# Building the decay masks and the query factors on the chip instead of loading them

## The chip, the cores and the metric

The kernel runs on one core of a Trainium2 chip. The metric is the device time of one execution in microseconds (us), lower is better. A profile of one execution gives the span of the core's work, engine by engine: PE is TensorE (its weight loads stand apart as PEld), DVE is VectorE, ACT is ScalarE, POOL is GpSimd, SP is the engine whose queue issues most DMAs. ACT has a DMA queue of its own.

## What is computed

The input is one attention-like layer ("retention": no softmax, a decay per head) and two feed-forward layers behind it, all in float32.

```python
# q, k, v: 4 batches x 8 heads x 576 positions x 64
gamma = 1.0 - 2.0 ** (-5.0 - arange(8))               # one decay per head
rel = pos[:, None] - pos[None, :]
Dmat = where(rel >= 0, gamma[:, None, None] ** rel, 0.0)
x = ((q @ k.T) / sqrt(64) * Dmat) @ v                 # 2304 tokens x 512
h = x @ w_in;   x = maximum(0.01 * h, h) @ w_out      # 512 -> 2048 -> 512
h = x @ w_in2;  x = (h - tanh(h)) @ w_out2
```

## The kernel before

The first stage, `retention()`, takes about the first 150 us; the two feed-forward layers, `layers()`, take the rest. Everything below on the change lies in the first 30 us of `retention()`.

The 8 heads are taken two at a time, so there are 4 batches x 4 pairs of heads = 16 steps, which this text numbers 0 to 15; step i uses head pair i mod 4. A step cuts the 576 positions into four chunks of 128 and a tail of 64. Within a chunk it forms the scores k.q (`scores`, L595, tile `sc`), multiplies them by the causal decay mask of the two heads (`mask`, L609, on DVE, into `pt`), and multiplies by v (`outputs_near`, L671). What earlier chunks contribute goes through a running state: k times v per chunk (`states_mm`, L628, tile `x_c`; k is first scaled by `kt_sb` in `prep_k`, L576, on ACT), added up with the heads' decay on DVE (`states`, L636 and L638), and multiplied by q (`outputs_far`, L660), where q has been multiplied by its own decay factors `qt_sb` in `prep_q` (L565 and L570, on POOL). The tail's scores are L601 and its mask L618.

The constants come from the host as three tables: the masks `cmask` (128 x 4 pairs x 2 x 128 floats, 128 KB a pair), q's factors `qtab` (64 KB a pair) and `ktab` (4 KB). Pair 0's part of the first two is loaded on ACT's queue at the start, the parts of pairs 1 to 3 on SP's queue in steps 0 to 2, ahead of the loads of q, k and v (L827, L828).

The order on each engine is the order in which the code is written (the schedule is manual), and every engine runs its instructions in that order. A DMA completes on one of eight semaphores, taken in turn; the issue of a DMA whose semaphore is still in use waits for the earlier DMA. There is one `sc` buffer, so the scores of step i+1 wait until DVE has read those of step i. From step 5 on, each step also does a piece of the first feed-forward layer (`unit_h`, L721; `unit_o`, L746). The weights for that are loaded from step 0 on into the not yet used end of `acc` and narrowed from float64 words on ACT, DVE and POOL (`fill`: L152, L158, L163, L169, L242, L243), a few instructions in each step.

A float32 matmul of the program is two records of the trace (8 score products are "x16"), one in the reduced float32r form is one record.

Of the kernel before, what the change touches and what calls it, by code (L numbers as in the profile page):

```python
# [10 lines left out]
F32 = mybir.dt.float32  # L11
# [3 lines left out]
AF = mybir.ActivationFunctionType  # L15
ALU = mybir.AluOpType
PSUM = bass.MemoryType.PSUM

P = 128
CH = 128  # L20
# [15 lines left out]
def retention_moe_moe(  # L36
# [7 lines left out]
    w1o: bass.AP,  # L44
    w2i: bass.AP,
    w2o: bass.AP,
    cmask: bass.AP,
    qtab: bass.AP,
    ktab: bass.AP,
    out: bass.AP,  # L50
    gamma: list,
# [1 line left out]
    nc = tc.nc  # L53
    B, NP, _, S = qT.shape
    NT, DM = out.shape
    NF = w1i.shape[0]
    KK = DM // P
# [21 lines left out]
    acc_t = acc.rearrange("p (d t) -> p d t", d=KK)  # L79
# [15 lines left out]
    QW, EARLY = 256, 6  # L95
# [421 lines left out]
    def retention():  # L517
        with ExitStack() as ac:
            ak = ac.enter_context(tc.tile_pool(name="ak", bufs=1))
# [4 lines left out]
            ps_a = ac.enter_context(tc.tile_pool(name="ps_a0", bufs=1, space=PSUM))  # L524
# [3 lines left out]
            x_b = ps_s.tile([P, 2, QW], F32, name="x_b")  # L528
# [4 lines left out]
            cm_sb = ak.tile([P, NP, 2, CH], F32, name="cm_sb")  # L533
            qt_sb = ak.tile([P, NP, CH], F32, name="qt_sb")
            kt_sb = ak.tile([P, NP, 2], F32, name="kt_sb")
            sts = [ak.tile([P, NFULL, 64], F32, name=f"st{i}") for i in range(2)]
            decay = ak.tile([P, NP], F32, name="decay")
            pt_ = [ak.tile([P, 2, S], F32, name=f"pt{i}") for i in range(2)]
            bds = [ak.tile([P, 2, TAIL], F32, name=f"bd{i}") for i in range(2)]
            qk, kv, pts = {}, {}, {}  # L540
            order = [(b, p) for b in range(B) for p in range(NP)]

            def load(i):
                load_qk(i)
                load_v(i)
# [32 lines left out]
            def prep_tail(i):  # L578

                q = qk[i][:, 1, MAIN:]  # L580
                for h in range(2):
                    o = slice(64 * h, 64 * h + 64)
                    if i:
                        nc.scalar.activation(out=bds[i % 2][o, h, :], in_=q[o], func=AF.Copy)
                    else:
                        nc.vector.tensor_copy(out=bds[i % 2][o, h, :], in_=q[o])
# [109 lines left out]
            def fill(i, part):  # L696
                a, b = marks[i:i + 2] if i < len(order) else marks[-1:] * 2
                now = a + (b - a) * (part + 1) // 3
                for op in ops[done[0]:now]:
                    op()  # L700
                done[0] = max(done[0], now)
# [66 lines left out]
            def pair_steps(i, fast):  # L768

                nonlocal u  # L770
                if fast:
                    unit_h(u)
                    fill(i, 1)
                    if u:
                        unit_o(u - 1)
                        unit_evac(u - 1)
                    u += 1
                if i:
                    ot = o_place(i - 1)
                    outputs_far(i - 1, ot, range(1, NFULL))  # L780
                    outputs_near(i - 1, ot, range(NFULL))
                    outputs_far(i - 1, ot, [NFULL])
                    outputs_near(i - 1, ot, [NFULL])
                    del qk[i - 1]
                    del pts[i - 1], kv[i - 1]
                if i < len(order):
                    states_mm(i)
                    scores_tail(i)
                    states(i)
                if i:  # L790
                    finish(i - 1, x_t, MAIN, S)
                    finish(i - 1, ot[:, :MAIN], 0, MAIN)
                if i < len(order):
                    mask_tail(i)
                if i + 1 < len(order):
                    prep_tail(i + 1)
                    prep_k(i + 1)

            t = ap_.tile([P, 2, S], F32, tag="qk", name="qk")
            nc.sync.dma_start(out=t[:, 1, :], in_=qT[0, 0])  # L800
            nc.scalar.dma_start(out=cm_sb[:, 0], in_=cmask[:, 0])
            nc.sync.dma_start(out=t[:, 0, :], in_=kT[0, 0])
            qk[0] = t
            nc.scalar.dma_start(out=kt_sb, in_=ktab)
            nc.scalar.dma_start(out=qt_sb[:, 0, :], in_=qtab[:, 0, :])
            load_v(0)
            load_qk(1)
            load_v(1)
# [9 lines left out]
            for p in range(NP):  # L818
                for h in range(2):
                    nc.vector.memset(  # L820
                        decay[64 * h:64 * h + 64, p:p + 1], float(gamma[2 * p + h] ** CH)
                    )
            prep_tail(0)
            prep_k(0)
            for i in range(len(order)):
                if i + 1 < NP:
                    nc.sync.dma_start(out=cm_sb[:, i + 1], in_=cmask[:, i + 1])  # L827
                    nc.sync.dma_start(out=qt_sb[:, i + 1, :], in_=qtab[:, i + 1, :])  # L828
                if i + 2 < len(order):
                    load(i + 2)  # L830
                if i < 2:
                    load_piece(pieces[i + 1])
                fast = i >= first
                sc = scores(i)
                prep_q(i)
                mask(i, sc)
                fill(i, 0)
                pair_steps(i, fast)
                fill(i, 2)
            pair_steps(len(order), True)  # L840
            assert done[0] >= len(ops)
# [222 lines left out]
```

## Time and profile before

| | |
|---|---|
| median of 3 runs | 876.88 us (876.71 to 878.21) |
| the profiled execution's own time | 876.76 us |
| its span | 875.0 us |
| PE, busy share of the span | 98% |
| DVE, ACT, POOL, busy share | 67%, 51%, 42% |
| stages | about 150 us retention with pieces of the first layer, then the two layers |

The profile is of one execution, whose own time is 1.76 us longer than its span. In its chain of the work that ended last, PE has 89% of the span. The shares are means over stages: the change touches only the start, which has to be read by itself.

### The profile page before, as it was taken

The numbers are of one execution on the slowest core, as the hardware profiler recorded it, in microseconds if no ns is written. First come the engines' busy times: TensorE is split into PE (matmuls) and PEld (weight loads), VectorE is DVE, ScalarE is ACT, GpSimd is POOL, SyncE is SP. The second block draws the span as 40 slices with busy tenths as digits, with TensorE's granted clock in tenths as the row PEclk, the third lists the DMA queues.
The fourth block names the chain that finished last, engine by engine and source line by source line (L and its number), as shares of the span: only waits on it lengthen the run. The fifth ranks groups of instructions, "written<-read, shape, count | busy, mean of one in ns | idle before, by whom it ended". The sixth has DMA issues, their size and how long they took to land.

```text
span 875.0 us, 14820 instructions
## 1 busy us (share of the span) xinstructions
PE 857.5 (98%) x5584; PEld 744.8 (85%) x5584; DVE 587.6 (67%) x1006; ACT 445.6 (51%) x888; POOL 365.0 (42%) x297
## 2 busy tenths in 40 slices
PE   6999999999999999999999999999999999999997
PEld 5889999888988888888888888888898889889886
DVE  5996776687685777658745567754666566656665
ACT  4553454453345334454534566665666556665663
POOL 2642222140046203273334756554455545453553
PEclk9999999999999999999999999999999999999999
DMA  9835663333455433654534200260004300261112
GB/s 336 316 120 181 207 206 133 133 120 121 145 193 209 153 120 108 230 193 114 208 111 145 97 1 1 73 211 7 1 25 146 119 1 1 73 217 49 49 49 73
DMA packets 36471, 109.23 MB, mean 125 GB/s; under 512 B 4144, under 2 KB 5680, under 8 KB 36400
## 3 DMA queue, kind: packets, MB, share of 16 engines
q1 hardware_dynamic: 35968, 108.08, 35.9%
q8 instruction: 44, 0.72, 0.3%
q10 hardware_dynamic: 432, 0.20, 0.1%
q14 instruction: 27, 0.22, 0.1%
HBM read 78.39 MB, written 29.88 MB: 124 GB/s over the span
## 4 chain that ended last, share of the span: by engine, by line
PE 89%; DVE 5%; DMA 2%; issue 1%; POOL 1%; ACT 1%; SPq 0%; POOLq 0%; DVEq 0%; ACTq 0%
PE a L404 40%; PE h L262 26%; PE h L296 12%; PE a L746 3%; PE x_b L721 3%; PE o L671 1%; DMA cm_sb<-in_cmask 1%; PE sc L595 1%; PE o L660 1%; DVE cw L169 1%; DMA acc<-in_w1i 1%; DVE pt L609 1%; PE x_c L628 0%; DVE acc L467 0%; DVE xl L482 0%
## 5 line engine op out<-in xcount | busy, mean ns | idle before, releaser
L262 PE MATMUL h<-xh,wi 128*128 128x512 f32 (+1 forms) x800 | 229.7, 356 | 0.0
L404 PE MATMUL a<-wp,g 128*128 128x512 f32 x864 | 220.4, 393 | 0.9 <-POOL g L376 0.5
L404 PEld LDWEIGHTS a<-wp,g 128*128 128x128 f32 x864 | 154.5, 188 | 29.5 <-POOL g L376 1.2
L243 POOL TENSOR_TENSOR wi<-cw,wi 128x512 fp32r<-128x512 f32 x64 | 89.8, 1420 | 214.0 <-ACT wi L242 188.3
L404 PE MATMUL a<-g,wp 128*128 128x512 f32 (+1 forms) x816 | 175.9, 364 | 0.6 <-DVE g L376 0.6
L404 PEld LDWEIGHTS a<-g,wp 128*128 128x128 f32 x816 | 141.4, 189 | 25.6 <-DVE g L376 0.8
L262 PEld LDWEIGHTS h<-xh,wi 128*128 128x128 f32 x800 | 143.6, 188 | 22.5
L262 PE MATMUL h<-xl,wi 128*128 128x512 f32 (+1 forms) x400 | 142.4, 356 | 0.0
L350 POOL TENSOR_TENSOR v<-t,u 128x512 f32<-128x512 f32 (+1 forms) x76 | 92.4, 1216 | 92.4 <-ACT t L347 90.5
L376 POOL TENSOR_TENSOR g<-v,g 128x512 fp32r<-128x512 f32 (+1 forms) x76 | 95.7, 1259 | 80.8 <-ACT g L375 80.8
L336 ACT ACTIVATE g<-h 128x512 fp32r<-128x512 f32 (+1 forms) x68 | 37.2, 548 | 166.4 <-PE h L262 124.5
L169 DVE SCALAR_TENSOR_TENSOR cw<-st,cw 128x512 uint32<-128x512 uint32 x112 | 99.0, 884 | 2.9
L370 DVE SCALAR_TENSOR_TENSOR v<-q,v 128x512 f32<-128x512 f32 (+1 forms) x76 | 54.7, 720 | 49.9 <-POOL v L350 49.6
L262 PEld LDWEIGHTS h<-xl,wi 128*128 128x128 f32 x400 | 75.5, 189 | 11.4
L467 DVE TENSOR_TENSOR acc<-a,acc 128x512 f32<-128x512 f32 (+1 forms) x114 | 70.9, 658 | 21.0 <-PE a L404 21.0
L375 ACT ACTIVATE g<-v 128x512 fp32r<-128x512 f32 (+1 forms) x76 | 45.4, 597 | 75.5 <-DVE v L373 68.1
L346 ACT ACTIVATE u<-h 128x512 f32<-128x512 f32 (+1 forms) x80 | 44.0, 550 | 78.0 <-DVE h L290 53.9
L296 PE MATMUL h<-xh,wi 128*128 128x256 f32 x384 | 75.6, 281 | 0.5 <-DVE v L373 0.3
L369 DVE TENSOR_TENSOR h<-h,t 128x512 f32<-128x512 f32 (+1 forms) x80 | 51.5, 644 | 33.7 <-ACT t L347 32.9
L158 DVE TENSOR_SCALAR cw<-cw 128x512 f32<-128x512 f32 x64 | 34.1, 533 | 57.8 <-ACT cw L152 57.7
L296 PEld LDWEIGHTS h<-xe,wi 128*128 128x128 f32 x432 | 60.2, 188 | 8.5 <-DVE mk L290 2.4
L296 PEld LDWEIGHTS h<-xh,wi 128*128 128x128 f32 x384 | 61.9, 188 | 2.9 <-DVE v L373 1.8
(86 smaller groups left out, 1244.5 us busy)
## 6 DMA issues: line engine op xcount, KB each, us to landing
kept<-wi SPq DMA_DIRECT2D x48, 512.0 KB, 3.9
wi<-kept SPq DMA_DIRECT2D x32, 512.0 KB, 4.6
st<-in_w2o SPq DMA_DIRECT2D x16, 512.0 KB, 5.9
st<-in_w2i SPq DMA_DIRECT2D x16, 512.0 KB, 3.7
wp<-kept SPq DMA_DIRECT2D x16, 512.0 KB, 3.7
st<-in_w1i SPq DMA_DIRECT2D x12, 512.0 KB, 4.3
st<-in_w1o SPq DMA_DIRECT2D x12, 512.0 KB, 3.4
kv<-in_vn SPq DMA_DIRECT2D x16, 320.0 KB, 5.3
```

Of the source, the lines that this page charges most:

```text
L169: nc.vector.scalar_tensor_tensor(out=t["w"], in0=t[src], scalar=scalar, in1=t["w"], op0=op, op1=ALU.bitwise_or)
L243: nc.gpsimd.tensor_tensor(out=wp[:, 1, :], in0=wf, in1=wp[:, 0, :].bitcast(F32), op=ALU.subtract)
L262: nc.tensor.matmul(out=ps[:, :n], lhsT=w[:, wi, cs], rhs=x[:, kk, t0:t0 + n], start=kk == 0 and i == 0, stop=kk == KK - 1 and i == 2,)
L296: nc.tensor.matmul(out=out_, lhsT=w[:, wi_, at:at + P], rhs=x(xi, kk), start=start and kk == 0 and j == 0, stop=stop and kk == 1 and j == ...
L346: nc.scalar.activation(out=u[:, :n], in_=h, func=AF.Square)
L350: nc.gpsimd.tensor_tensor(out=v[:, :n], in0=t_[:, :n], in1=u[:, :n], op=ALU.mult)
L369: nc.vector.tensor_tensor(out=h, in0=h, in1=t_, op=ALU.subtract)
L370: nc.vector.scalar_tensor_tensor(out=v, in0=q, scalar=RHO_A, in1=v, op0=ALU.add, op1=ALU.mult)
L375: nc.scalar.activation(out=gt[:, 0, :n], in_=v, func=AF.Copy)
L376: (nc.gpsimd if m else nc.vector).tensor_tensor(out=gt[:, 1, :n], in0=v, in1=gt[:, 0, :n].bitcast(F32), op=ALU.subtract)
L404: nc.tensor.matmul(out=o, lhsT=l, rhs=r, start=f == 0 and i == 0 and d % pack == 0, stop=f == GF - 1 and i == 2 and (d + 1) % pack == 0, s ...
L467: nc.vector.tensor_tensor(out=dst, in0=a, in1=dst, op=ALU.add)
```

## The change

The host no longer sends the finished masks and factors. It sends `rows`, 2 x 4 pairs x 640 floats (20 KB): for each head of a pair gamma to the power -r, gamma to the power r (with the scale, and with zeros in the other head's place), gamma to the power 128+r, and a row of ones and zeros that picks the head. It also sends `causal`, one 128 x 128 table of ones and zeros (64 KB) for all heads. On the chip, a matmul over the two rows gives the uncut mask of a pair (128 x 256), DVE multiplies it by `causal` into `cm_sb`, a second matmul (128 x 128) gives q's factors, and ACT copies them into `qt_sb`. `tables` does that for pairs 0 and 1 before step 0, and for pairs 2 and 3 at the end of step 0. The products use the accumulators that the feed-forward pieces use later (`tab` in the pool of `a`, `tab_q` in `x_b`). `rows` is loaded into a part of `acc` that is not yet in use. The DMAs of `cmask` and `qtab` on both queues are gone.

```diff
+            row = acc_t[:2, :NP, :5 * CH]
+            tab = ps_a.tile([P, KK, QW], F32, tag="a", name="tab")
+            tab_q = x_b.rearrange("p i (j c) -> p (i j) c", c=CH)
...
+            def tables(ps):
+                for p in ps:
+                    nc.tensor.matmul(
+                        out=tab[:, p, :], lhsT=row[:, p, :CH], rhs=row[:, p, CH:3 * CH],
+                        start=True, stop=True,
+                    )
+                    nc.tensor.matmul(
+                        out=tab_q[:, p, :], lhsT=row[:, p, 4 * CH:], rhs=row[:, p, 3 * CH:4 * CH],
+                        start=True, stop=True,
+                    )
+                for p in ps:
+                    nc.vector.tensor_tensor(
+                        out=cm_sb[:, p], in0=tab[:, p, :].rearrange("p (h r) -> p h r", h=2),
+                        in1=up_sb.to_broadcast([P, 2, CH]), op=ALU.mult,
+                    )
+                    nc.scalar.activation(out=qt_sb[:, p, :], in_=tab_q[:, p, :], func=AF.Copy)
...
             nc.sync.dma_start(out=t[:, 1, :], in_=qT[0, 0])
-            nc.scalar.dma_start(out=cm_sb[:, 0], in_=cmask[:, 0])
+            nc.scalar.dma_start(out=row, in_=rows)
+            nc.scalar.dma_start(out=up_sb, in_=causal)
             nc.sync.dma_start(out=t[:, 0, :], in_=kT[0, 0])
             qk[0] = t
             nc.scalar.dma_start(out=kt_sb, in_=ktab)
-            nc.scalar.dma_start(out=qt_sb[:, 0, :], in_=qtab[:, 0, :])
...
+            tables(range(2))
             prep_tail(0)
             prep_k(0)
             for i in range(len(order)):
-                if i + 1 < NP:
-                    nc.sync.dma_start(out=cm_sb[:, i + 1], in_=cmask[:, i + 1])
-                    nc.sync.dma_start(out=qt_sb[:, i + 1, :], in_=qtab[:, i + 1, :])
...
                 pair_steps(i, fast)
+                if i == 0:
+                    tables(range(2, NP))
                 fill(i, 2)
```

The order on PE at the program's start, before the change: the scores of step 0 (`sc`), the state products (`x_c`), the tail's scores (`x_e`), and the scores of step 1. The brackets name the semaphores waited for; DMAHW with a digit is one of the eight of the DMAs.

```order
L595 MATMUL sc<-qk 128x128 [waits DMAHW3_49,DMAHW1_49]
L595 MATMUL sc<-qk 128x128 x7
L628 MATMUL x_c<-kv 64x64 [waits DMAHW6_49,DMAHW5_49,Activation_49]
L628 MATMUL x_c<-kv 64x64 [waits Activation_49]
L628 MATMUL x_c<-kv 64x64 x6
L601 MATMUL x_e<-bd_106,qk 128x128 [waits DVE_49]
L595 MATMUL sc<-qk 128x128 [waits DMAHW0_49,DMAHW7_49,DVE_49,PE_49]
```

The same place after the change, where the lines of the program have moved by 21 (scores are L616, state products L649, the tail L622):

```order
L549 MATMUL tab<-acc 128x256 [waits DMAHW0_49]
L553 MATMUL x_b<-acc 128x128
L549 MATMUL tab<-acc 128x256
L553 MATMUL x_b<-acc 128x128
L616 MATMUL sc<-qk 128x128 [waits DMAHW2_49,DMAHW1_49]
L616 MATMUL sc<-qk 128x128 x7
L649 MATMUL x_c<-kv 64x64 [waits DMAHW4_49,DMAHW3_49,Activation_49]
L649 MATMUL x_c<-kv 64x64 x6
L622 MATMUL x_e<-bd_108,qk 128x128 [waits DVE_49]
L549 MATMUL tab<-acc 128x256
L553 MATMUL x_b<-acc 128x128
L616 MATMUL sc<-qk 128x128 [waits DMAHW5_49,DMAHW7_49,DVE_49,PE_49]
```

Four table products now stand ahead of the scores of step 0, behind the arrival of `rows` (DMAHW0), and four more ahead of the scores of step 1.

The order on ACT at the program's start, its DMA issues among it, before the change:

```order
L801 DMA cm_sb<-in_cmask 128x256
L804 DMA kt_sb<-in_ktab 128x8
L805 DMA qt_sb<-in_qtab 128x128
L813 ACT_TABLE_LOAD
L813 ACTIVATE qb<-qb 128x1 [waits DVE_49]
L576 ACTIVATE kv<-kv,kt_sb 128x4x64 [waits DMAHW5_49,DMAHW2_49]
```

And after the change:

```order
L822 DMA acc<-in_rows 2x4x640
L823 DMA up_sb<-in_causal 128x128
L826 DMA kt_sb<-in_ktab 128x8 [waits DMAHW0_49]
L834 ACT_TABLE_LOAD
L834 ACTIVATE qb<-qb 128x1 [waits DVE_49]
L562 ACTIVATE qt_sb<-x_b 128x128 [waits PE_49]
L562 ACTIVATE qt_sb<-x_b 128x128
L597 ACTIVATE kv<-kv,kt_sb 128x4x64 [waits DMAHW3_49,DMAHW0_49]
```

The issue of `ktab` now waits for the semaphore of `rows`, and with it everything behind it on ACT; the two copies of q's factors stand ahead of `prep_k` (L576 before, L597 now).

## Rows read from the trace of the kernel before

**Rows 1.** The page's busy times of the engines over the span.

```profile
PE 857.5 (98%) x5584; PEld 744.8 (85%) x5584; DVE 587.6 (67%) x1006; ACT 445.6 (51%) x888; POOL 365.0 (42%) x297
```

**Rows 2.** Chain that ended last, 0 to 75 us: start, us, what.

```profile
11.78 6.20 DMA cm_sb<-in_cmask
...
18.07 1.29 DVE pt L609 x2
...
28.85 1.29 DVE pt L609 x2
...
58.62 0.42 PE x_e L601 x2
```

**Rows 3.** Busy time by stretch; the last three columns: PEclk, DMA share, GB/s.

```profile
2.00:3.00 1.00, 0.00 (x0) 0.00 (x0) 0.13 (x3) 0.85 (x1) 0.00 (x0) 1.00 0.80 87
...
5.00:10.00 5.00, 4.52 (x48) 4.08 (x50) 2.29 (x7) 1.89 (x6) 1.54 (x2) 1.00 1.03 378
...
25.00:30.00 5.00, 4.14 (x70) 3.35 (x68) 4.85 (x11) 3.50 (x10) 4.44 (x5) 1.00 1.03 383
```

**Rows 4.** Timeline, 0 to 20 us: start, us, engine, line, instructions, idle before.

```profile
0.74 0.41 ACTq L801 DMA_DIRECT2D cm_sb<-in_cmask  x1
...
1.17 0.46 ACTq L804 DMA_DIRECT2D kt_sb<-in_ktab  x1
...
5.48 2.08 PE L595 MATMUL sc<-qk 64*128 64x128 f32 x16 [5.48 <-DMA qk<-in_kT]
...
6.31 0.91 ACT L576 ACTIVATE kv<-kv,kt_sb 128x256 f32<-128x256 f32 x2 [2.67 <-DMA kv<-in_kn]
...
7.49 1.12 PE L628 MATMUL x_c<-kv 128*64 128x64 f32 x16
7.60 1.29 DVE L609 TENSOR_TENSOR pt<-sc,cm_sb 128x512 f32<-128x512 f32 x2 [2.58 <-PE sc L595]
...
8.54 0.65 PE L601 MATMUL x_e<-bd,qk 128*128 128x128 f32 x2
...
9.12 1.16 PE L595 MATMUL sc<-qk 64*128 64x128 f32 x16
...
10.21 0.87 PE L660 MATMUL o<-qk,st 64*64 64x128 f32 x12
...
12.18 1.29 DVE L609 TENSOR_TENSOR pt<-sc,cm_sb 128x512 f32<-128x512 f32 x2 [2.03 <-DMA cm_sb<-in_cmask]
...
13.03 0.49 PE L601 MATMUL x_e<-bd,qk 128*128 128x128 f32 x2
...
13.40 0.91 DVE L638 SCALAR_TENSOR_TENSOR st<-st,decay,x_c 128x64 f32<-128x64 f32 x3
...
16.31 0.69 DVE L169 SCALAR_TENSOR_TENSOR cw<-acc,cw 128x512 uint32<-128x512 uint32 x1
...
18.07 1.29 DVE L609 TENSOR_TENSOR pt<-sc,cm_sb 128x512 f32<-128x512 f32 x2 [1.07 <-DMA cm_sb<-in_cmask]
```

**Rows 5.** DMA issues: KB each, us from issue to landing.

```profile
cm_sb<-in_cmask ACTq DMA_DIRECT2D x1, 128.0 KB, 4.0
...
kt_sb<-in_ktab ACTq DMA_DIRECT2D x1, 4.0 KB, 4.3
```

**Rows 6.** Groups by form, 0 to 35 us: busy us, mean ns, idle before.

```profile
L618 DVE TENSOR_TENSOR pt<-x_e,cm_sb 64x128 f32<-64x128 f32 x5 | 1.5, 295 | 0.1
...
L576 ACT ACTIVATE kv<-kv,kt_sb 128x256 f32<-128x256 f32 x12 | 5.4, 500 | 3.7 <-DMA kv<-in_kn 3.6
...
L636 ACT ACTIVATE st<-x_c 128x64 f32<-128x64 f32 x5 | 1.1, 220 | 6.3 <-issue 4.1 <-PE x_c L628 2.1
```

**Rows 7.** All waits of PE: us in total, times, longest.

```profile
PE sc L595 <- DMA qk<-in_kT: 7.9, 4, 5.5
PE sc L595 <- DVE pt L609: 1.1, 1, 1.1
```

More of the change, by code (lines that the diff above doesn't have):

```diff
@@ L46, in retention_moe_moe @@
     w2o: bass.AP,
-    cmask: bass.AP,
-    qtab: bass.AP,
+    rows: bass.AP,
+    causal: bass.AP,
     ktab: bass.AP,
@@ L535, in retention @@
             kt_sb = ak.tile([P, NP, 2], F32, name="kt_sb")
+            up_sb = ak.tile([P, 1, CH], F32, name="up_sb")
+            row = acc_t[:2, :NP, :5 * CH]
+            tab = ps_a.tile([P, KK, QW], F32, tag="a", name="tab")
+            tab_q = x_b.rearrange("p i (j c) -> p (i j) c", c=CH)
             sts = [ak.tile([P, NFULL, 64], F32, name=f"st{i}") for i in range(2)]
@@ L1037 @@
     rel = r[None, :] - r[:, None]
-    row_gamma = np.repeat(gamma.reshape(NP, 2), D, axis=1).T
     back = gamma ** -r[:, None].astype(float)
-    mask = np.where(rel >= 0, gamma[:, None, None] ** rel * scale, 0.0)
+    by_pair = [a.reshape(CH, NP, 2).transpose(2, 1, 0) for a in (
+        back, gamma ** r[:, None] * scale, gamma ** (CH + r[:, None]) * scale,
+    )]
+    down, right, far = by_pair
+    two = np.zeros((2, NP, 2, CH))
+    two[0, :, 0], two[1, :, 1] = right[0], right[1]
+    pick = np.zeros((2, NP, CH))
+    pick[0, :, :D], pick[1, :, D:] = 1.0, 1.0
     consts = {
-        "cmask": mask.reshape(NP, 2, CH, CH).transpose(2, 0, 1, 3),
-        "qtab": row_gamma[:, :, None] ** (CH + r) * scale,
+        "rows": np.concatenate([down, two.reshape(2, NP, 2 * CH), far, pick], axis=2),
+        "causal": (rel >= 0)[:, None, :],
         "ktab": back.reshape(CH, NP, 2),
```

## The prediction

> **What bounds the kernel now.** I read the page's busy times first: PE is busy 98% of the span [rows 1], so over the whole the kernel is bound by PE, and a change elsewhere counts only through the places where PE starts late. The list of PE's waits says where these are: 7.9 us in four waits for k's loads, one of them the 5.5 us before the first score product, and one of 1.1 us for DVE's mask [rows 7]. So I then read the chain that ended last, in its first 75 us. It goes through the load of a mask, which takes 6.20 us and lands at 17.98, into the mask multiplication of step 2 at 18.07; from there to the mask of step 4 at 28.85 every piece of the chain is DVE, with gaps of 0.03 us [rows 2]. The end of that mask at 30.14 frees the score buffer, and that is PE's 1.1 us wait for a mask, the only one of its kind [rows 7]. The busy times by stretch agree: in 25 to 30 us DVE is busy 4.85 of 5 us [rows 3]. The reader is to see that the first 18 us hang on loads, the next 12 on DVE and the rest on PE, and that what moves the start of step 2's mask moves the end by the same amount: neither DVE's work up to 30 us nor PE's work after it is touched by the change.
>
> So the whole question is at what time step 2's mask starts: 18.07 before. It followed a DVE instruction that ended at 16.31 + 0.69 = 17.00 and then waited 1.07 us for its table [rows 4]. Without the table's DMA it could have started at 17.00, if all in front of it stayed.
>
> **What is removed.** Eight DMAs, 4 x (128 + 64) KB = 768 KB, against 84 KB that come in their place. The DMA engines move 378 to 383 GB/s between 5 and 30 us, with a busy share of 1.03 [rows 3], so they are full, and 684 KB less are 1.8 us of their time, 0.5 us for each step's tables. DVE waits for masks twice, 3.1 us in all: 2.03 before step 1's mask and 1.07 before step 2's [rows 4]. Only the second stands directly on the chain. After the first, DVE does step 1's mask and then has to wait for the state products on PE anyway: they are issued by 13.03, where the tail's scores follow, and DVE's state sums start at 13.40 [rows 4]. So the first wait costs nothing as long as PE is as it was.
>
> **What is added, and where it lies.** ACT gets four copies of 128 x 128: between 0.22 us (128 x 64) and 0.50 (128 x 256) [rows 6], I take 0.3. DVE gets four multiplications of 128 x 256: between 0.295 (64 x 128) [rows 6] and 0.65 (128 x 512, half of 1.29 [rows 4]), I take 0.42. The first two lie in the idle 2.58 us before step 0's mask, the other two in the 2.03 us before step 1's [rows 4]; there they cost nothing unless the products that feed them are late. What is left is PE, which has the products in its order ahead of the scores of step 0 and of step 1, where before it had no gap at all between the scores of step 0 and the tail's scores of step 1.
>
> One call of `tables` is two products of 256 columns and two of 128, six units of 128 columns. No row shows such a product alone. The nearest from below: eight score products of 128 columns take 10.21 - 9.12 = 1.09 us, 0.136 each [rows 4], but they use half the array's height each, and two heads go side by side. From above: the tail's scores, one product of 128 columns at full height, take 0.42 to the next start [rows 2], with a change of shape behind it. I take 0.25, near twice the lower: 1.5 us a call (bounds 0.8 and 2.5).
>
> The first call runs when PE is slow. The profile's granted clock is 1.00 (2.4 GHz) everywhere in the first 30 us [rows 3], yet the first score products last 2.08 us and the next step's, the same ones, 1.16 [rows 4]: the records are those of the lower level (1.2 GHz) until somewhere between 8.54 and 9.12 us. By start to start the ratio is (7.49 - 5.48) / 1.09 = 1.84, so the first call takes 2.8 us.
>
> When can it start? `rows` is issued first on ACT's queue, as step 0's mask was, at 0.74 [rows 4]. That DMA of 128 KB landed 4.0 us later [rows 5], at 4.7; in 2 to 3 us the engines moved only 87 KB [rows 3], so nothing lands before 2.8. Twenty KB should land sooner than 128, among the same transfers: I take 4.1. The Trainium skill bears on it, "DMA: Bandwidth & Descriptors", "Why a DMA increments its semaphore by 16 and not by 1": a DMA from such a queue is spread over the largest number of engines up to 16 that divides the slowest dimension on both sides, which is 2 for a tile of two partitions. By that rule, with a sixteenth of 383 GB/s for each engine, 10 KB an engine take 0.43 us alone and 0.85 beside SP's transfers, an estimate that no row here shows; it speaks against a landing before 3.2, and the sum would not change.
>
> **The walk on PE.** First call 4.1 to 6.9. Scores of step 0 from 6.9 (before: 5.48): between 1.1 and 2.0 us, I take 1.5, to 8.4. ACT has its two copies at 6.9 to 7.5 and then scales k in 0.9 us [rows 4], to 8.4, so the state products start at 8.5 (before: 7.49) and take 0.6, then 0.4 for the tail's scores, to 9.5. Second call 1.5: step 1's scores start at 11.0 instead of 9.12, 1.9 later. From there to the tail's scores of step 1 nothing changes (3.91 us, 9.12 to 13.03 [rows 4]), nor in DVE's run from 13.40 to 17.00. So step 2's mask starts at 17.00 + 1.9 = 18.9 instead of 18.07: 0.8 us later. The loads for it come earlier than before and don't bind. The sum: 876.76 (the profiled execution's own time) + 0.8 = **877.6 us**; that execution is 0.12 below the median of 876.88. In a formula: the loss is the delay of step 1's scores less 1.07.
>
> Bounds by the same formula. Low: `rows` at 3.7, 0.136 a unit (1.5 us slow), scores at 5.4 and already fast (1.1), k scaled from 6.3 to 7.2, 0.5 + 0.4, then 0.8: step 1's scores at 8.9, a gain of 1.3, 875.4. High: 0.42 a unit, below.
>
> **Rivals.** A change under 0.2% (1.75 us) can hardly be told from none: faster ends at 875.1, slower begins at 878.6.
>
> *The waits come back in full.* DVE gets its 3.1 us back, less 0.84 for the two multiplications that fall into the first wait: 876.76 - 2.3 = 874.5. For it speak the full DMA engines. Against it: PE has to do the second call before step 1's scores, and to be 0.2% faster these have to start by 9.12 + 1.07 - 1.75 = 8.4, 0.5 before my lower bound. What could do that is an earlier fast level: PE begins at 4.1 instead of 5.48, and all records up to 9.1 are slow ones, so up to 0.9 us on the scores and 0.5 on the state products. The Trainium skill, "TensorE: Matmul & The Clock Gate", "The HAM clock gate (the "warmup" mystery)", says that half rate is the default and activity on PE releases it; by that rule the early products bring the rise forward, and the records here, slow first and fast later, agree with it. Chance 0.10.
>
> *The new wait on ACT decides (slower).* `ktab`'s issue now waits for `rows`, to 4.1 instead of 1.17 [rows 4]. Where it took 4.3 us to land [rows 5], it lands at 8.4, and k's scaling runs to 9.3; the state products start 0.8 later than in my walk: 878.4. It decides as soon as `ktab` lands after 7.5. For me it comes faster, since the masks' 128 KB no longer stand ahead of it in its queue. Chance 0.17.
>
> *The products cost what the tail's scores cost (slower).* 0.42 a unit is 4.6 us for the first call and 2.5 for the second: 8.7, scores (fast) 9.8, 10.7 with what follows, step 1's scores at 13.2, 4.1 late: 876.76 + 4.1 - 1.07 = 879.8. Chance 0.11.
>
> **How the numbers follow.** My walk, give or take what its middle values allow (876.2 to 878.6), has 0.62; the three rivals 0.10, 0.17 and 0.11. Faster by over 0.2% is the first alone: 0.10. Slower is the last, half of the second and the walk's upper edge: 0.25. The rest, 0.65, is within 0.2%. The range goes from the lower bound, 875.4, to the dearest products, 879.8; what lies outside is most of the first rival and a little above the last.
>
> **What would show it.** Right, if the first table product starts near 4.1 and step 1's scores near 11; if step 2's mask starts with no wait for a DMA, behind DVE's own work, at 18.5 to 19.3; and if the masks of steps 2 and 4 stay 10.8 us apart. Wrong, if step 1's scores start before 10 (cheap products or an early fast level), if ACT sits idle for `ktab` before it scales k, or if the 10.8 us change, since then the table's loads had cost DVE or PE something beyond their own waits.

## The result, and the profile after

| | before | after |
|---|---|---|
| median | 877.99 us (6 runs, 876.71 to 878.21) | 884.13 us (6 runs, 883.47 to 885.07) |
| the profiled execution's own time | 876.76 | 884.02 |
| its span | 875.0 | 881.9 |

The changed kernel is slower: ratio 1.0075, 95% interval 1.0062 to 1.0088. The 877.6 us forecast is 6.5 us too low, and the time lies above the range. The span grew by 6.9 us, and this is the difference to look for.

The page's busy line of the kernel after, against [rows 1]: PE has 16 records more and is busy 7.8 us longer, while DVE and ACT gained about 1 us each and POOL nothing.

```profile
PE 865.3 (98%) x5600; PEld 751.0 (85%) x5600; DVE 588.7 (67%) x1010; ACT 446.4 (51%) x892; POOL 365.0 (41%) x297
```

So the start has to be read again. The timeline of the kernel after (start, us, engine, line, instructions, idle before), against [rows 4]:

```profile
0.74 1.26 ACTq L822 DMA_DIRECT2D acc<-in_rows  x1
...
4.02 0.33 ACTq L826 DMA_DIRECT2D kt_sb<-in_ktab  x1
...
4.04 1.22 PE L549 MATMUL tab<-acc 2*128 2x256 f32 x2 [4.04 <-DMA acc<-in_rows]
...
6.90 2.08 PE L616 MATMUL sc<-qk 64*128 64x128 f32 x16
...
9.02 1.29 DVE L630 TENSOR_TENSOR pt<-sc,cm_sb 128x512 f32<-128x512 f32 x2 [0.64 <-PE sc L616]
...
10.23 0.91 ACT L597 ACTIVATE kv<-kv,kt_sb 128x256 f32<-128x256 f32 x2 [2.78 <-DMA kt_sb<-in_ktab]
...
10.79 1.52 PE L649 MATMUL x_c<-kv 128*64 128x64 f32 x16 [1.81 <-ACT kv L597]
12.24 0.80 PE L622 MATMUL x_e<-bd,qk 128*128 128x128 f32 x2
...
12.96 1.22 PE L549 MATMUL tab<-acc 2*128 2x256 f32 x2
...
15.82 2.08 PE L616 MATMUL sc<-qk 64*128 64x128 f32 x16
...
17.83 1.54 PE L681 MATMUL o<-qk,st 64*64 64x128 f32 x12
17.95 1.29 DVE L630 TENSOR_TENSOR pt<-sc,cm_sb 128x512 f32<-128x512 f32 x2 [1.69 <-PE sc L616]
...
21.95 0.91 DVE L659 SCALAR_TENSOR_TENSOR st<-st,decay,x_c 128x64 f32<-128x64 f32 x3 [2.72 <-ACT st L657]
...
26.09 1.29 DVE L630 TENSOR_TENSOR pt<-sc,cm_sb 128x512 f32<-128x512 f32 x2
```

Three things stand in these rows. The first call runs from 4.04 to 6.90, as forecast to 0.06 us. Then PE stands still for 1.81 us, because ACT cannot scale k: it waits 2.78 us for `ktab`, whose issue stood behind the arrival of `rows`. And nothing that PE does up to 19 us is fast: the same scores that took 1.16 us from 9.12 on [rows 4] take 2.08 at 6.90 and again at 15.82, the far products 1.54 instead of 0.87. The state products take 1.52 where 0.64 is their fast duration, but not all of that is the level: in experiment 1, at the slow level and with `ktab` in time, they take 1.12, and the other 0.40 is the second half of k, which ACT scales only from 10.64 on. Before, the records were fast from about 9 us. After, the first records of fast duration stand at 20.6.

The stretches of the kernel after (columns as in [rows 3]):

```profile
5.00:10.00 5.00, 3.98 (x23) 3.21 (x21) 2.02 (x6) 1.32 (x4) 0.87 (x1) 1.00 0.96 333
...
15.00:20.00 5.00, 5.00 (x40) 4.13 (x40) 2.04 (x4) 0.99 (x3) 1.55 (x2) 1.00 0.11 43
```

From 15 to 20 us PE is busy all the time, for 40 records only, while the DMA engines stand nearly idle (share 0.11): PE frees no buffer, so SP, which issued a load at 10.26, issues its next at 21.00. So the slow records are not PE kept waiting by full DMA engines.

The column of the granted clock says 1.00 in both stretches, as it did before while the records were slow [rows 3]. That is not a reading of the level. The clock's own record in the trace has its first entry at 19.88 us in the kernel after and at 8.90 in the kernel before, full speed (2.4 GHz) in both, and the column counts what lies ahead of the first entry as 1.00. These two times are the ones at which the durations of equal records change. Where a record falls back after its first entry, the column does show the lower level (1.2 GHz): it reads 0.50 in experiments 8 and 10, with the same long durations.

The chain that ended last of the kernel after (start, us, what), against [rows 2]:

```profile
4.02 6.18 DMA kt_sb<-in_ktab
10.23 0.52 ACT kv L597
10.79 1.52 PE x_c L649 x16
...
13.03 1.15 PE tab L549 x2
...
15.89 2.01 PE sc L616 x16
...
26.24 4.57 DMA kv<-in_kn
30.82 1.29 DVE pt L630 x2
...
35.83 1.30 DVE pt L630 x2
37.22 1.16 PE sc L616 x16
```

The mask's load is out of the chain; `ktab`'s load, the second call and slow scores are in it. The load of k at 26.24 landed at 30.81, while DVE's own work ahead of step 3's mask ended at 30.80, so neither decides there alone. The masks of steps 2, 3 and 4 start at 26.09, 30.82 and 35.83, before at 18.07, 23.00 and 28.85: step 2's is 8.0 us late, step 4's 7.0. The scores after it start at 37.22, before at 30.24: 6.98 us late, and that is the span's 6.9. The row of the kernel before for these scores:

```profile
30.24 1.16 PE L595 MATMUL sc<-qk 64*128 64x128 f32 x16 [1.10 <-DVE pt L609]
```

The list of PE's waits of the kernel after (us in total, times, longest), against [rows 7]:

```profile
PE tab L549 <- DMA acc<-in_rows: 4.0, 1, 4.0
PE x_c L649 <- ACT kv L597: 1.8, 1, 1.8
```

PE waits less at its start than before (4.0 instead of 5.5). This list alone would have called the change a gain; the loss is in PE's busy time.

### The profile page after: what moved, and what is told of

It reads as the page before. It is cut to its first block, busy times and chain, and to the rows that moved or that the text cites. A ratio compares the mean times of both kernels' runs of the same rounds, so it can differ in the third digit from the quotient of the medians.

```text
span 881.9 us, 14857 instructions
## 1 busy us (share of the span) xinstructions
PE 865.3 (98%) x5600; PEld 751.0 (85%) x5600; DVE 588.7 (67%) x1010; ACT 446.4 (51%) x892; POOL 365.0 (41%) x297
## 4 chain that ended last, share of the span: by engine, by line
PE 92%; DVE 3%; DMA 2%; POOL 1%; issue 1%; ACT 1%; POOLq 0%; DVEq 0%; ACTq 0%
PE a L404 39%; PE h L262 26%; PE h L296 12%; PE a L767 4%; PE x_b L742 3%; PE sc L616 2%; PE o L692 2%; PE o L681 1%; DMA kv<-in_kn 1%; PE x_c L649 1%; DMA kt_sb<-in_ktab 1%; PE x_e L622 1%; DVE acc L467 0%; DVE xl L482 0%; DVE v L370 0%
## 5 line engine op out<-in xcount | busy, mean ns | idle before, releaser
L169 DVE SCALAR_TENSOR_TENSOR cw<-st,cw 128x512 uint32<-128x512 uint32 x112 | 99.6, 889 | 2.9
L262 PEld LDWEIGHTS h<-xl,wi 128*128 128x128 f32 x400 | 75.5, 189 | 11.2
L158 DVE TENSOR_SCALAR cw<-cw 128x512 f32<-128x512 f32 x64 | 33.7, 526 | 56.7 <-ACT cw L152 56.6
```

The source lines that it names most:

```text
L169: nc.vector.scalar_tensor_tensor(out=t["w"], in0=t[src], scalar=scalar, in1=t["w"], op0=op, op1=ALU.bitwise_or)
L262: nc.tensor.matmul(out=ps[:, :n], lhsT=w[:, wi, cs], rhs=x[:, kk, t0:t0 + n], start=kk == 0 and i == 0, stop=kk == KK - 1 and i == 2,)
```

## The experiments

Ten kernels ran, two of them a second time for another profile. The theories that the expectations speak of: **A**, PE's records stay at the slow level longer, and the table products, with two of the array's 128 rows, do not bring the fast level; **B**, the wait for `ktab` alone (the gap on PE, and what follows from it) is the loss; **C**, the loads, which come at other times, cost the rest. "Before" in a ratio is the kernel before on the same chip in the same rounds: 878.15 us for experiments 1, 2, 4 and 7, 877.57 for 3, 5, 6 and 8, 877.06 for 9, 10 and the two second runs. These three groups ran on three chips, so kernels of different groups are compared by their ratios. "The level rises" below means the entry of full speed in the trace's clock record.

**1. `ktab` on SP's queue, in the changed kernel.** The wait for `rows` is gone, all else stays.

```diff
-            nc.scalar.dma_start(out=kt_sb, in_=ktab)
+            nc.sync.dma_start(out=kt_sb, in_=ktab)
```

> The changed kernel with one edit: ktab is issued on SP's queue behind k's first load, so that its issue no longer waits for rows. In the changed kernel the state products of step 0 started at 10.79 us, the scores of step 1 at 15.82, and PE's records were slow (1.2 GHz) until about 19 us; the time was 884.1. Theory A (two causes, each with its own price: the wait for ktab, and two-row table products that do not bring PE to its fast level): the state products start near 9.0, the scores of step 1 near 13.5 to 14, the records are still slow up to there, the gain is 1.8 to 2.5 us, about 882. Theory B (PE's gap in front of the late state products is what kept the records slow): both go at once, the records are fast from about 8 to 9 us, the scores of step 1 start near 12, and the gain is 5 us or more, 878 to 879. Theory C (the loads' later issue is what costs): the mask of step 2 stays 2 us or more behind the place that PE's order gives it, and the gain is under 1 us.

Measured: 882.43 us (median of 10), ratio 1.0045 (1.003 to 1.006). `ktab` landed 3.4 us after its issue, ACT and PE no longer waited for it. But the ten times fall into two groups: 878.61 and 878.75, and eight from 881.3 to 883.05. The profile is of the 878.75 one, so the same kernel was run once more for a profile of the other kind.

> The changed kernel with ktab's issue on SP once more, for a profile of an execution near its median of 882.4 (the one profile so far was of an execution of 878.75, with fast records from 10.2 us). Theory A: in an execution of 882 and more the second call takes about 2.9 us and step 1's scores 2.08, with no idle time for ktab; step 2's mask starts at about 24. Theory B: in such an execution PE is idle somewhere in the first 12 us by 3 to 4 us more than in the other.

It took 883.1 us. The timeline in the execution of 878.75, PE's start of step 1 and DVE's mask of step 2:

```profile
10.18 0.49 PE L622 MATMUL x_e<-bd,qk 128*128 128x128 f32 x2
10.60 0.69 PE L549 MATMUL tab<-acc 2*128 2x256 f32 x2
...
12.10 1.16 PE L616 MATMUL sc<-qk 64*128 64x128 f32 x16
...
20.51 1.29 DVE L630 TENSOR_TENSOR pt<-sc,cm_sb 128x512 f32<-128x512 f32 x2
```

And in the execution of 883.1, the same program:

```profile
9.00 1.12 PE L649 MATMUL x_c<-kv 128*64 128x64 f32 x16
10.05 0.80 PE L622 MATMUL x_e<-bd,qk 128*128 128x128 f32 x2
10.78 1.22 PE L549 MATMUL tab<-acc 2*128 2x256 f32 x2
...
13.63 2.08 PE L616 MATMUL sc<-qk 64*128 64x128 f32 x16
...
24.80 1.29 DVE L630 TENSOR_TENSOR pt<-sc,cm_sb 128x512 f32<-128x512 f32 x2
```

Up to the tail's scores at 10.1 the two agree to 0.15 us, and neither has a gap. Then one has fast records and the other slow ones: the level rises at 10.21 us in the one and at 19.78 in the other. Step 2's mask starts at 20.51 in the one and at 24.80 in the other, 4.29 us apart; the times are 4.35 apart. This is shown within one program, so no placement, load or wait of the change is in it: the level alone is worth 4.3 us here. The two profiles are of two chips, but the ten times that fall into two groups are of one chip. B falls, since eight of ten executions without the gap lie around 882.4, and so does C as the cause of these 4.3.

**2. `ktab` late in the kernel before, first attempt.** Its issue moved behind ACT's tanh.

> The kernel before with one edit: ktab's issue stands behind ACT's first activation, at about 3.7 us instead of 1.17. It has no table products. If a small DMA takes its turn behind all bytes that SP issued before it, it lands near 8.5 to 9 and the state products of step 0 start 2 us later than the 7.49 of before. Theory A: PE's gap of 2 us by itself does little to the level, the records are fast from 9 to 10 us on; step 1's scores start near 11, less the 1.07 us that step 2's mask waited anyway: 0.8 to 1.2 us slower than before. Theory B: the gap keeps the records slow to 13 us or later, and the loss is 3 us or more.

Measured: 877.02 us, ratio 0.999 (0.998 to 1.0). The edit did not do what it was made for: ACT's queue issued the DMA at 1.73, ahead of the end of the tanh at 3.16, and k was scaled at 6.41, as before. What it gave is another thing: in its profile (877.06 us) the scores of step 1 were slow (9.22 to 11.2) where [rows 4] has them fast, at the same time, and the level rises at 11.25 instead of 8.90. So without a table product, too, the moment differs, here by 2.4 us; but DVE had to wait for step 1's table until 12.40 anyway, and that wait covered the slow scores.

**3. `ktab` late in the kernel before, second attempt.** Its issue on SP behind `load_qk(1)`.

```diff
-            nc.scalar.dma_start(out=kt_sb, in_=ktab)
...
             load_qk(1)
+            nc.sync.dma_start(out=kt_sb, in_=ktab)
```

> The kernel before with ktab on SP's queue behind the loads of step 1, where its issue waits for a semaphore of the eight as it does in the changed kernel. The edit of the run before this one did not delay it. Here it should land near 9 to 10.5 us, and no table product is there. Theory A (the wait is worth its length less the 1.07 us that step 2's mask waited before, and the level of PE's records is another matter): the state products of step 0 start 2.5 to 3.3 us later than 7.49, the time is 1.5 to 2.5 us above before. Theory B (the gap on PE also keeps the records slow): the records are slow past step 1's scores, 3.5 us or more above before. Theory C (the wait is covered by DMA-bound loads): the same as before.

Measured: 879.61 us, ratio 1.0027 (1.0016 to 1.0038). PE's timeline:

```profile
9.49 1.51 PE L628 MATMUL x_c<-kv 128*64 128x64 f32 x16 [2.11 <-ACT kv L576]
...
11.66 2.08 PE L595 MATMUL sc<-qk 64*128 64x128 f32 x16
```

`ktab` landed at 8.9, PE stood 2.11 us, and the level rises at 14.34. The wait alone, with what followed it, costs the kernel before 2.0 us in the median: a third of the loss, not all of it.

**4. The second call at full height.** The four products of pairs 2 and 3 run over 128 rows of `kv[0]` instead of two rows of `rows`; these pairs' tables are not the kernel's. The call is changed as below, and `tables` takes the new source as an argument.

```diff
-                    tables(range(2, NP))
+                    tables(range(2, NP), kv[0].rearrange("p c d -> p (c d)"))
```

> The changed kernel, where the four products of the second call of tables read 128 rows of step 0's k in place of the two rows (the tables of pairs 2 and 3 are then not the right ones); number, columns and place of the products stay. Theory A (two rows do not count for PE's level): the records turn fast within the second call or right behind it, the scores of step 1 take 1.1 to 1.3 us instead of 2.0, the far products 0.8 instead of 1.47; gain 1.5 to 3 us, 881 to 882.5. Theory B and C: the records turn fast at the same 19 us as in the changed kernel, and the time is the same 884 within 0.7.

Measured: 881.74 us, ratio 1.0041 (1.0025 to 1.0056), against 1.0075 (1.0062 to 1.0088) of the changed kernel, with the wait for `ktab` still there (1.85 us). PE's timeline:

```profile
13.36 1.06 PE L550 MATMUL tab<-kv 128*128 128x256 f32 x2
...
14.64 0.97 PE L550 MATMUL tab<-kv 128*128 128x256 f32 x2
15.45 0.39 PE L555 MATMUL x_b<-kv 128*128 128x128 f32 x2
15.77 1.16 PE L618 MATMUL sc<-qk 64*128 64x128 f32 x16
```

Products of the same columns, in the same place: the level rises at 15.40, within them, the last takes 0.39 instead of 0.63, and step 1's scores are fast.

**5. and 6. Four products added to the kernel before**, behind step 0's tail, with two rows (`[:2]`) and with 128 (`[:128]`) and the columns of `tables`; their results are not used. The edit with two rows, its matmul calls joined into two lines each here; the two lines that make `tab` and `tab_q` are left out:

```diff
                 pair_steps(i, fast)
+                if i == 0:
+                    src = kv[0].rearrange("p c d -> p (c d)")[:2]
+                    for p in (2, 3):
+                        nc.tensor.matmul(out=tab[:, p, :], lhsT=src[:, :CH],
+                                         rhs=src[:, CH:3 * CH], start=True, stop=True)
+                        nc.tensor.matmul(out=tab_q[:, p, :], lhsT=src[:, :CH],
+                                         rhs=src[:, 3 * CH:4 * CH], start=True, stop=True)
```

> The kernel before with the second call's four products alone, over two rows of step 0's k and v, in the same place (behind the tail's scores of step 0), their results used by nothing; all tables still come by DMA. Theory A (two-row products do not lift PE's level): where the fast level has not come by 9.1 us it comes only behind step 1's scores; the products take 1.4 us fast or 2.8 slow, so step 1's scores start at 10.6 to 12; less 1.07, 0.4 to 3 us slower than before, with a spread between runs of 2 us or more. Theory B: fast as in the kernel before, products 1.4 us, 0.3 to 0.5 us slower.

> As the run with two rows, but over all 128 rows of the same tile: same number, columns and place of products. Theory A: the fast level comes within these products at the latest, step 1's scores are always fast; 0.4 to 1.5 us slower than before, and 1 us or more faster than the two-row run in the median. Theory B: the same time as with two rows within 0.4 us.

Measured: two rows 880.94 us, ratio 1.0035 (1.0021 to 1.0048); 128 rows 878.05, ratio 1.001 (0.9999 to 1.0021). Nothing else differs, and 2.9 us lie between the medians: nine of the ten times with two rows (879.81 to 882.4) are longer than all ten with 128 (876.46 to 879.62). In the profile with 128 rows (878.49 us) the products themselves are still slow, and the level rises at 12.66, in step 1's scores. One of the ten times with two rows was 876.6, and that is the one that the profile fell on; in it the products are fast and the whole call takes 1.5 us. So it was looked at again for a usual execution.

> The kernel before with four two-row products behind step 0's tail once more, for a profile of an execution near its median of 880.9 (the one profile so far was of an execution of 876.6, with fast products). Theory A: in such an execution the products take 2.7 to 2.9 us, step 1's scores 2.08, and the far products 1.5; step 2's mask starts at 21 to 23 with no wait for a DMA. Theory B: products of 1.5 us, and the time lost at a load or on DVE.

This missed its aim: it took 876.56 us, again one with fast products (9.01 to 10.51). How a usual execution of it loses its 3 to 4 us is so not seen in a profile. What the second profile does show is the forecast's arithmetic:

```profile
10.51 1.16 PE L597 MATMUL sc<-qk 64*128 64x128 f32 x16
...
18.42 1.29 DVE L611 TENSOR_TENSOR pt<-sc,cm_sb 128x512 f32<-128x512 f32 x2
```

Step 1's scores start 1.39 us later than in [rows 4]; step 2's mask starts 0.35 later and behind DVE's own work; 1.39 less the wait of 1.07 is 0.32. In both profiles the level rises ahead of the products (8.32 and 8.69), and two-row products do not bring it down again.

**7. More work for PE ahead of the first call**, in the changed kernel: six full-height products of 128 columns from 0.99 us on.

```diff
+            nc.gpsimd.memset(ones, 1.0)
+            for _ in range(6):
+                nc.tensor.matmul(out=tab[:, 0, :CH], lhsT=ones, rhs=ones, start=True, stop=True)
             tables(range(2))
```

> The changed kernel with six more products of 128 columns at full height, over a constant tile, ahead of the first call of tables, in the time in which PE waits for rows (about 1.3 to 4 us). ktab lands as late as in the changed kernel, so the state products cannot start before 10.7. Theory A: the records are fast by 5 to 8 us; if they stay so over the gap, step 1's scores start near 13.3 and the gain is 4 us, near 880; if the gap lets them fall back, the gain is near none. Theory B: with the gap in place they are slow behind it, and the gain is under 1 us.

Measured: 883.93 us, ratio 1.0065 (1.0049 to 1.0082), no gain. PE's timeline:

```profile
0.99 2.93 PE L847 MATMUL tab<-ones 128*128 128x128 f32 x12 [0.99 <-POOL ones L845]
...
6.77 2.08 PE L617 MATMUL sc<-qk 64*128 64x128 f32 x16
10.83 1.52 PE L650 MATMUL x_c<-kv 128*64 128x64 f32 x16 [1.98 <-ACT kv L598]
...
15.86 2.08 PE L617 MATMUL sc<-qk 64*128 64x128 f32 x16
```

PE has work without a break from 0.99 to 8.85 and everything is slow; the level rises at 20.31. So "PE was not at work early enough" is not the cause, and theory A's hope of the fast level by 8 us failed here. Starting earlier did not help; the products just behind it are again the two-row ones.

**8. Two pairs loaded, two made.** Pairs 0 and 1 by DMA as before; `rows` and `causal` on SP in step 0; the products of pairs 2 and 3 behind step 1's tail.

```diff
             for i in range(len(order)):
+                if i == 0:
+                    nc.sync.dma_start(out=cm_sb[:, 1], in_=cmask[:, 1])
+                    nc.sync.dma_start(out=qt_sb[:, 1, :], in_=qtab[:, 1, :])
+                    nc.sync.dma_start(out=row, in_=rows)
+                    nc.sync.dma_start(out=up_sb, in_=causal)
...
-                if i == 0:
+                if i == 1:
                     tables(range(2, NP))
```

> A version that could beat both: pairs 0 and 1 come by DMA as before, rows and causal go on SP's queue in step 0, and only pairs 2 and 3 are made by products, behind the tail's scores of step 1, where PE waited 0.7 us for a load before. Nothing is added ahead of step 1's scores. Theory A: step 2's mask no longer waits 1.07 us for its DMA but gets 0.8 us of the new multiplications on DVE in front of it: 0.3 to 0.8 us faster than before, not to be told from it. Theory C (the loads are what counts): 1.5 us or more faster, since 0.3 MB fewer are loaded. Rival: two-row products keep PE slow here too: 1 us slower.

Measured: 880.61 us, ratio 1.0039 (1.0026 to 1.0052). It is not the repair that it was meant to be. `rows` goes into `acc`, where `fill` has its weights; on SP its issue waited for one of these, in the waits of SP's queue:

```profile
SPq L852 <- DMA acc<-in_w1i: 4.6, 1, 4.6
```

and step 2's loads stood behind it. On PE:

```profile
14.89 0.69 PE L551 MATMUL tab<-acc 2*128 2x256 f32 x2 [0.86 <-DMA acc<-in_rows]
...
17.66 2.08 PE L618 MATMUL sc<-qk 64*128 64x128 f32 x16 [1.20 <-DMA qk<-in_kT]
```

The level rises at 10.36; behind the four two-row products and in a gap of 1.20 us it falls, at 17.19, and it rises again at 24.01. The stretch between (columns as in [rows 3]) has the lower clock in its column:

```profile
18.00:24.00 6.00, 6.00 (x58) 5.00 (x58) 4.05 (x8) 1.24 (x4) 1.99 (x2) 0.50 1.01 383
```

**9. and 10. Where the second call stands**, with `ktab` on SP in both. In the one, pairs 2 and 3 are made behind step 1's tail instead of step 0's. In the other, moreover, only pair 0 is made ahead of step 0's scores and pair 1 behind step 0's tail. The first one's edit beside that of experiment 1:

```diff
-                if i == 0:
+                if i == 1:
                     tables(range(2, NP))
```

The second kernel's:

```diff
-            tables(range(2))
+            tables(range(1))
...
-                if i == 0:
-                    tables(range(2, NP))
+                if i < 2:
+                    tables(range(i + 1, 2 * i + 2))
```

> The changed kernel with ktab's issue on SP's queue (as in the second undoing before) and the second call of the products moved from behind step 0's tail to behind step 1's, where it is needed one step later. Theory A (what is left of the loss is the time that PE's records stay at the slow level, and two-row products neither lift it nor count as work): step 1's scores follow step 0's tail directly, start at about 10.7 and rise there as they do in the kernel before; the second call, at about 15, costs 1.5 us in PE's slack against DVE or a little more: 878.5 to 880. Theory B (the products' own time and the wait for ktab are all there is): the call's 1.5 to 2.9 us leave the chain before step 1's mask, the first call's 1.4 remain: 877.5 to 878.5. If the late products throw the records back to the slow level as in the run with two pairs by DMA, step 2's scores last 2.08 us: 880 to 882.

> As the run before it in this batch (ktab's issue on SP), but the first call makes only pair 0's products, pair 1's stand behind step 0's tail, and those of pairs 2 and 3 behind step 1's. Step 0's scores start at about 5.6 as in the kernel before (products 4.1 to 5.5), two products of 0.8 to 1.4 us stand ahead of step 1's scores. Theory A: the scores of step 0 start on time, but the two products ahead of step 1's scores hold the records low or not from run to run: 878 to 880.5, and above the kernel before. Theory B: step 2's mask 0 to 0.5 us later than before, within 0.2% of before: 877 to 878.3. DMA rival (684 KB less give something back once the path is as before): 876 to 877.

Measured: 879.35 us (878.23 to 879.79), ratio 1.0021 (1.0012 to 1.0031), and 880.4 (878.92 to 881.5), ratio 1.0033 (1.002 to 1.0046). PE's timeline of the first:

```profile
10.84 2.08 PE L616 MATMUL sc<-qk 64*128 64x128 f32 x16
...
16.20 0.69 PE L549 MATMUL tab<-acc 2*128 2x256 f32 x2
...
17.70 1.16 PE L616 MATMUL sc<-qk 64*128 64x128 f32 x16
```

Its level rises at 13.12. The same four products take 1.5 us instead of 2.9, because they stand where the records are already fast, the level does not fall behind them, and the spread to 883 is gone: ratio 1.0021 against 1.0045 of experiment 1, which is 2.1 us, as A expected. In the profile of the second (879.08 us), step 0's scores start at 5.84, nearly as before, and step 1's at 10.59, fast, after a rise at 9.91; but the level falls at 16.74, just behind the two-row products of pairs 2 and 3 (step 2's scores take 1.83, the far ones 1.54), and rises again at 20.15. A stretch between (columns as in [rows 3]):

```profile
17.00:20.00 3.00, 3.00 (x28) 2.44 (x28) 2.93 (x5) 0.41 (x3) 1.61 (x2) 0.50 1.00 365
```

PE had no gap there. In this second kernel step 2's mask starts at 20.13, 2.06 later than before, and that can be worked out: step 1's scores are 1.47 late, and between them and step 2's mask DVE now has two multiplications of tables (0.76) and an L169 of 1.76 us instead of 0.69; that is 3.3, less the 1.07 of the wait 2.2. The hope that fewer bytes on the DMA engines would give something back (876 to 877) failed. Of the kernels that made tables on the chip, none had a median under the kernel before's.

## Why the prediction was wrong, step by step

**Right.** That only the start counts, up to step 2's mask: a delay there of 8.0 us became 6.98 at the end (the missing 1.0 is below). That the first call starts near 4.1 and takes 2.8 (4.04 and 2.86). That `rows` does not land before 3.2 (by the queue's rule, cited in the prediction; landed at 4.0, which decides nothing about that rule's figure). The price of the products at the fast level: 0.25 us a unit, 1.5 a call, a choice between 0.136 and 0.42 and so in part luck; in experiment 1's execution of 878.75 the second call takes 1.50 (10.60 to 12.10). That DVE's waits for the masks' loads go, and that the formula holds, delay of step 1's scores less 1.07, where the records are fast (experiment 6's second profile: 0.32 worked out, 0.35 measured).

**Wrong: the level.** The step that failed is the walk's "second call 1.5", with the fast scores and state products around it: it took the records to be fast from about 8.5 us on, as in the one profile before. The level rose at 19.88 instead of 8.90. The terms that were too small for it, read from the timeline (the 1.05 from experiment 1's execution of 883.1, 9.00 to 10.05):

| | walk | after |
|---|---|---|
| scores of step 0 to where state products could start | 1.6 | 2.0 |
| state products without a wait for k, then the tail's scores | 0.6 + 0.4 | 1.05 + 0.72 |
| second call | 1.5 | 2.86 |
| start of step 1's scores to DVE's state sums | 4.28 | 6.13 |

These are 4.4 us together, and the experiment that had the two levels in one program gave 4.3. The prediction had read from the rows that the first call would be slow, and had the price of a slow call (2.8). It took the column's 1.00 for 2.4 GHz, which is no reading ahead of the record's first entry, but went by the durations, rightly. It did not ask what would happen if the level rose later: it treated a time of the trace before as a fixed date. It did ask the opposite, an earlier rise through earlier work; that rival is refuted by this profile and by experiment 7. Even where the level rose at 10.21, in experiment 1, step 1's scores start at 12.10, 1.1 us behind the walk: step 0's scores and state products were slow there too.

**Wrong: `ktab`.** This was a rival with 0.17: the new wait on ACT, `ktab` landing at 8.4 and 0.8 us lost. The mechanism was right. It landed at 10.20, 6.2 us after its issue, next to the load of k that SP had issued at 3.71 (landed 6.7 us later, at 10.4): 4 KB on ACT's queue did not pass it. PE lost 1.9 us of wait, and 0.4 more in the state products, whose second half waited for the second half of k. The Trainium skill, "DMA: Bandwidth & Descriptors", "Queues, rings and completion order", says that a DMA's completion on an engine is written only after all earlier writes of that engine, those of its other queues too; the 6.2 us agree with it, against 3.4 on SP's queue, issued at 1.65, in experiment 1. No run separates that rule from plain crowding.

**The sum.** The level's terms are 4.4, `ktab` 2.3; DVE's own run to step 2's mask took 4.14 instead of 3.60, 0.5; from there to step 4's mask 9.74 instead of 10.78, a gain of 1.0. That is 6.2 above the walk's 877.6, 883.8, against 884.02 of the profiled execution. The gain of 1.0 is L169, in the groups of DVE between the two masks (columns: busy, mean ns, idle before), before and after:

```profile
L169 DVE SCALAR_TENSOR_TENSOR cw<-acc,cw 128x512 uint32<-128x512 uint32 x3 | 3.1, 1038 | 0.0
```

```profile
L169 DVE SCALAR_TENSOR_TENSOR cw<-acc,cw 128x512 uint32<-128x512 uint32 x3 | 2.1, 698 | 0.0
```

The prediction had said that these 10.8 us would stay, since DVE's work there is not touched by the change; the lengths of the instructions changed with their place. In the rows the long ones stand beside work of POOL: before, 1.30 us at 27.05, with POOL busy from 26.52 to 28.54; after, 0.68 at 27.29, with POOL idle from 25.04 to 28.77; in experiment 10, 1.76 at 18.45, with POOL busy from 18.39 to 20.38. One overlap did not lengthen it (after, 0.73 at 34.61, POOL from 34.75 to 35.52). The 0.5 of DVE's longer run is L158, 0.93 at 23.94 beside POOL's work of 23.31 to 25.04, against 0.43 at 15.39 with POOL idle. No run tried it apart.

A second count, by the start of step 2's mask in four profiles, goes the same way: before 18.07, the change with `ktab` on SP and an early rise 20.51 (+2.44), the same with a late rise 24.80 (+4.29), the change itself 26.09 (+1.29). These are 8.02 together. The wait is worth 1.3 in this count, less than its 2.3 above: the level rises at 19.8 with it and without it, so with it less of step 1 is slow (6.13 us from its scores to DVE's state sums, 7.05 in experiment 1's late execution). In experiment 3 the wait is worth 2.0.

**The rivals as such.** They were priced as alternatives, each inside the range. What came was the wait for `ktab` together with a late rise of the level, which was no rival at all. The second call looks like the rival of dear products (0.48 us a unit, against its 0.42), but at the fast level it takes 0.25: it was slow, not dear.

**Open.** What decides whether the level rises at 9 us or at 20. That it varies between executions of one program is shown. That the late rise goes with the four two-row products in their place ahead of step 1's scores rests on three comparisons: over 128 rows instead of two, in the changed kernel (ratio 1.0041 against 1.0075) and in the kernel before (878.05 us against 880.94), and moved one step later (1.0021 against 1.0045). But two of the ten executions of experiment 1, with the same products in that place, rose early by their times (one of them by its profile), and in experiment 3 the level rose at 14.34 with no such product. How two-row products would do it is not shown: behind them the level fell in two profiles (experiments 8 and 10) and stayed up in four (experiment 1's early one, the two of experiment 5, experiment 9), and experiment 7's full-height products had no effect. The Trainium skill, "TensorE: Matmul & The Clock Gate", "The HAM clock gate (the "warmup" mystery)", says that the clock is held back by default, that activity releases it, and that the moment varies from run to run. The variation agrees, and is large here (10.21 and 19.78 us in one program); that activity releases it does not tell this case's executions apart.

## What to carry to other kernels

Where a stage is read from one profile and its PE records change level in it, the moment of the change can differ from one execution to the next (10.21 and 19.78 us here): price the stage at both levels, at full length, before adding products to it, and add the rivals up where they can come together. A load wait that is removed may have been covering slow work behind it, so its return is at most what remains when that work is slow. A small table whose issue waited for another's arrival landed behind what had been queued meanwhile, 6.2 us after its issue; issued early on the queue that did not wait, it landed in 3.4.

## What the runs showed that was not expected

- ACT's issue of the DMA of two partitions (20 KB) took 1.26 us, that of 128 partitions in its place in the kernel before 0.41 [rows 4].
- `ktab`'s 4 KB landed 6.2 us after an issue at 4.02, and 4.3 us after one at 1.17 [rows 5].
- The granted clock column says 1.00 while equal products take 1.8 times as long, up to the first entry of the clock's record; behind it the column shows the lower level where there is one (0.50 in experiments 8 and 10).
- PE worked without a break for 7.9 us, 2.9 of them full-height products, and was at the slow level for another 11.5 us, with one gap of 1.98 (experiment 7).
- One program: the slow level ended at 10.21 us in one execution and at 19.78 in another, 4.35 us in the time; on one chip, two of its ten times lie with the first and eight nearer the second.
